# Attention and gated feed-forward on one core: end-of-group work moved between score tiles, row maxima turned on VectorE, weights marked as held

## The chip, the cores and the metric

The kernel runs on one core of one Trainium2 chip. The time of a run is the device time in microseconds (us) of one execution. The engines have the names of the profile: PE (TensorE matmuls), PEld (its weight loads), DVE (VectorE), ACT (ScalarE), POOL (GpSimd) and SP (SyncE, which here only issues DMAs).

## The reference, cut to what matters

```python
x = A_x                                            # 1 x 2048 x 512
mod = (silu(c) @ w_mod).reshape(1, 6, 1, -1)
sa, ca, ga, sb, cb, gb = (mod[:, n] for n in range(6))
h = layernorm(x) * (1 + ca) + sa
q = (h @ wq).reshape(B, S, 32, 16).transpose(0, 2, 1, 3)   # 32 heads of 16
k, v = h @ wk, h @ wv                              # one k and v for all heads
p = softmax(einsum("bhqd,bkd->bhqk", q, k) * 16 ** -0.5)
x = x + ga * (concat_heads(einsum("bhqk,bkd->bhqd", p, v)) @ wo)
h = layernorm(x) * (1 + cb) + sb
x = x + gb * ((sigmoid(h @ w_gate) * (h @ w_up)) @ w_down) # inner width 1792
```

All inputs and the output are float32.

## The kernel before, in words

**Units and steps.** Attention is cut into 32 units: 8 blocks of 256 queries by 4 groups of 8 heads. A unit has 16 steps, one for each block of 128 keys, so the main loop has 512 steps. A step has two half-steps (`for n in range(2)`).

**Scores are computed twice.** A `sa` tile (token `a`, functions `a_tile`, `a_product`, `a_max`) has 128 queries on the partitions and 512 keys along the row; DVE takes its row maximum into `mx`. There are 64 such tiles to a unit, 2048 in all, and they run ahead of the unit that needs them: `A0` of them are done before the main loop starts, and the loop does four per step. An `st` tile (`st_tile`) has 128 keys on the partitions and 512 (query, head) columns; ACT takes its exponential into `P`. The maximum is subtracted inside that product: the rows 48, 49, 112 and 113 of the unit's query tile `qp` hold the maximum, as a high and a low half-precision part, against constant rows of `kp`. So the maxima of a unit must have been turned from partitions into rows, and stored into `qp` by DMA, before the unit's first `st` tile.

**The two halves of the array.** A matmul of the loop uses 64 rows of the PE array and 32 columns; `columns` issues four of them to make 128 columns. In a half-step the two `sa` and the two `st` tiles use one row half (here: the scoring half), and the product of `P` with `V` (`pv`, output `craw`, float32, which runs as two passes) uses the other (the value half). The two halves swap these roles at every second change of step. The order written in a half-step is `ORDER`: `a0 s0 c a1 s1`, where `c` is `pv`.

**Couples.** All the other matrix products (the query projection `pq`, the output projection `po`, gate and up `pgu`, down `pd`) run as a `Couple` of two groups with one PSUM bank each. A couple is cut into parts by `plan`, and `piece` issues one part at the end of a half-step: mostly two terms, each on both row halves (16 matmuls). The last part of a couple calls `end` for both groups. For gate and up these are ACT's `th` (tanh) and DVE's `u` (a copy), for the others likewise one operation on ACT and one on DVE, or two on ACT. They free the couple's two banks, which the next couple needs for its first part, as a rule one half-step later.

**Banks.** PSUM has two banks for `st`, three for `sa`, two for couples and one for `craw`. An `st` tile therefore waits for the exponential of the tile two before it, an `sa` tile for the maximum of the tile three before it.

**Turning the maxima.** When a unit's 64 tiles are reduced, `max_end` (at the start of the next step) reduces `mx` once more in two DVE operations into `m16`; in the step after, `max_rows` turns it with a float32 matmul against `ident` into a bank taken from the `sa` ring, ACT copies it out twice (`m32`, `mh`), and at the end of that step `low` subtracts on DVE and issues four DMAs on SP's queue.

**Order.** Every instruction of PE, DVE, ACT and SP in the loop is kept in the order in which the code issues it (`Ordered`, `keep`). Before the loop a prologue runs from the hand-written list `PLAN`; there `a` issues an `sa` tile and `x` its maximum, `mx`, `my`, `mz` turn the maxima of unit 0.

Of the kernel before, what the change touches and what calls it, by code (L numbers as in the profile page):

```python
# [8 lines left out]
F16 = mybir.dt.float16  # L9
F32 = mybir.dt.float32  # L10
AF = mybir.ActivationFunctionType
ALU = mybir.AluOpType
# [4 lines left out]
P = 128  # L17
# [33 lines left out]
)  # L51

H32 = ('ADAD', 'AAAA', 'AAAA', 'AAAA')
HLO = ('PDPD', 'PPPP', 'PPPP', 'PPPP')

A0 = 84
ORDER = "a0", "s0", "c", "a1", "s1"
LAG = 2

# [37 lines left out]
def adaln_mqa_glu_kernel(  # L97
# [51 lines left out]

    def columns(dst, l_, r_, start, stop):
        for c_ in range(0, P, 32):
            pe.matmul(dst[c_:c_ + 32], l_[:, c_:c_ + 32], r_, start=start, stop=stop)

    turn, done, side, open_ = nc.alloc_semaphore("turn"), [0], [0], [False]
    pe.sem_clear(turn)
# [40 lines left out]
    class Couple:  # L198
# [3 lines left out]
        def part(self, n0, n1):  # L202
            if n0 == 0:
                for g in self.gs:
                    g.open()
            m = self.gs[0].n
            for n in range(n0, n1):
                if n == m:
                    assert self.since is not None or done[0] > self.marks
                    take_over(self.since)  # L210
                for j in (1 - side[0], side[0]):
                    g = self.gs[j ^ (n >= m)]
                    l_, r_, *cut = g.term(n % m, slice(64 * j, 64 * j + 64))
                    columns(cut[0](g.bank) if cut else g.bank, l_, r_, n == 0, n == 2 * m - 1)
                if n == m - 1:
                    self.since, self.marks = None, done[0]
                    if open_[0]:
                        hand_over()
                        self.since = done[0]
                if n in self.after:  # L220
                    self.after[n]()
            if n1 == self.n:
                for k, g in enumerate(self.gs):
                    g.end(g.bank, k == 1)
# [394 lines left out]
    pend, seen = [], {}  # L619

    def max_end(i):
        m16 = wp.tile([64, 32], F32, tag="m16", name="m16", bufs=4)
        for u in range(2):
            dve.tensor_reduce(m16.rearrange("p (h t u) -> p h t u", t=2, u=2)[:, :, :, u], mxs[i][64 * u:64 * u + 64],
                              axis=AX.X, op=ALU.max)
        return lambda: max_rows(i, m16)

    def max_rows(i, m16):
        qp = get_q(i)
        pm = sbank("sa")  # L630
        pe.matmul(pm[:32, :64], m16, ident[:64, :64], start=True, stop=True)
        m32 = wp.tile([32, 64], F32, tag="m32", name="m32", bufs=4)
        act.activation(m32, pm[:32, :64], AF.Identity, scale=1.0 / SM)
        mh = wp.tile([32, 2, 64], F16, tag="mh", name="mh", bufs=4)
        act.activation(mh[:, 0], m32, AF.Identity)

        def low():
            dve.tensor_tensor(mh[:, 1], m32, mh[:, 0], op=ALU.subtract)
            for h in range(2):
                for j in range(2):  # L640
                    r = 64 * j + 48 + h
                    sp1.dma_start(qp[r:r + 1], mh[16 * j:16 * j + 16, h, :])

        return low


    def st_tile(i, t, pr, j, second):
# [191 lines left out]
    def ffn_block(b, end_of_all=False):  # L839
# [63 lines left out]
        def gu_pair(p, t, m):  # L903
            def begin():
                if m == 0:
                    fetched(at + NDC * (p + 1) - 1)

            def term(n, rs):
                k, i = divmod(n, 3)
                h_, w_ = ((0, 0), (1, 0), (0, 1))[i]  # L910
                return h2[t][0][rs, 4 * h_ + k, :], gws[at + NDC * p + k][rs, 2 * w_ + m]

            def end(p_, second):
                if m == 0:
                    ths[p, t] = th = t32("th")
                    act.activation(th, p_, AF.Tanh, scale=0.5 / (SH * SW))
                    return
                u_ = t32("u")
                dve.tensor_copy(u_, p_)
                gated_rows(ths.pop((p, t)), u_, f"g{p}{t}")  # L920

            return Group("gu", 12, "pgu", term, end, begin)

        def gu_last(t):
# [5 lines left out]
            def term(n, rs):  # L930
                k, i = divmod(n, 3)
                gw = gws[at + NDC * NPR + k // 2].rearrange("p m n -> p (m n)")
                h_, w_ = ((0, 0), (1, 0), (0, 1))[i]
                c0 = (2 * (k % 2) + w_) * 512
                return h2[t][0][rs, 4 * h_ + k, :], gw[rs, c0:c0 + 512]

# [143 lines left out]
    def q_end(b, o):  # L1080
# [9 lines left out]
              "a": a_next, "x": lambda: a_max(*held.pop(0)), "mx": lambda: rows.append(max_end(0)), "my": lambda: rows.append(rows.pop()()), "mz": lambda: rows.pop()(),  # L1090
# [73 lines left out]
    def plan(s, hb):  # L1164
# [18 lines left out]
            at += z  # L1183
        assert at == g.n, (at, g.n, g.stage)

    def piece(s, h):
        plan(s, 2 * s + h)
        if run:
# [4 lines left out]


    vq = []
    lows = []

    for i, (b, o) in enumerate(units):
        if o == 0 and b > 0:
# [4 lines left out]
        for kb in range(NKB):  # L1204
# [5 lines left out]
            for z in [z for z in waits if z[0] <= s]:  # L1210
                waits.remove(z)
                z[1]()
            ready_rows, rows[:] = rows[:], [max_end(*z) for z in late]
            an = A0 + 4 * (s - kb % 2)
            second = kb % 2 == 1
            h = sides(kb)[second]

            for n in range(2):
                t = kb - kb % 2 + n
                for z in ORDER:  # L1220
                    k = int(z[1:] or 0)
# [12 lines left out]
            if second:  # L1234
                vq[:] = [(i, kb - 1), (i, kb)]
# [69 lines left out]
```

## Time and profile before

| | |
|---|---|
| time, median of 3 runs | 1634.7 us (1630.74 to 1636.57) |
| profiled execution, its own time | 1629.06 us |
| its span, first to last instruction | 1627.3 us |
| mean granted PE clock | 0.993 |
| PE, PEld busy | 1585.3 us (97%), 987.3 us (61%) |
| DVE, ACT, POOL busy | 1417.1 us (87%), 1288.7 us (79%), 666.2 us (41%) |
| main loop, first to last `st` matmul | 105.1 to 1535.5 us |

In a line of a group stand the code line, the engine, the operation, output and inputs, shapes and count, then busy time and mean duration, then idle time of the engine just before it. Nearly all work is issued through one helper, so its line is L143 and the tile names tell the groups apart. A timeline line has start and length in us; where several alike follow each other they are merged, with their count.

### The profile page before, as it was taken

The page shows a single profiled execution, that of the slowest core. Times are in us where ns is not written, and L with a number is a line of the kernel's source. Part 1 is how long each engine was busy: PE and PEld are TensorE (multiplying, and loading weights), DVE is VectorE, ACT ScalarE, POOL GpSimd, SP SyncE. Part 2 cuts the span into 40 slices and gives each one's busy share as a digit, 9 for nine tenths or more (in the row PEclk, how much of TensorE's full clock was granted, in tenths as well). Part 3 has the DMA queues.
Part 4 walks back from the last instruction along what each step waited for, and adds up shares of the span by engine and source line. Part 5 has one row for each costly group of instructions (what it writes and reads, how often), then busy time and mean ns, then how long its engine had stood idle before and what let it go on. Part 6 is the DMA issues. An engine that isn't in the chain of part 4 may idle for free.

```text
span 1627.3 us, 91846 instructions
## 1 busy us (share of the span) xinstructions
PE 1585.3 (97%) x41481; PEld 987.3 (61%) x41481; DVE 1417.1 (87%) x2400; ACT 1288.7 (79%) x2325; POOL 666.2 (41%) x827
## 2 busy tenths in 40 slices
PE   6899999999999999999999999999999999999998
PEld 3335554546666666666666666666666666665465
DVE  7789999999999999999999999999999999993041
ACT  4539998888888888888888888888888888888600
POOL 5453877244425332443226232543226322533223
PEclk9979999999999999999999999999999999999999
DMA  7122554044521233114321433115411343124411
GB/s 238 71 84 65 164 156 131 28 118 106 139 68 29 75 97 108 31 39 130 92 63 33 89 85 106 30 38 128 112 42 42 81 121 85 23 60 107 116 65 52
DMA packets 185076, 140.22 MB, mean 86 GB/s; under 512 B 96372, under 2 KB 144492, under 8 KB 184684
## 3 DMA queue, kind: packets, MB, share of 16 engines
q1 hardware_dynamic: 184684, 134.34, 30.4%
q8 instruction: 325, 5.32, 1.3%
q14 instruction: 67, 0.55, 0.1%
HBM read 97.18 MB, written 16.24 MB: 70 GB/s over the span
## 4 chain that ended last, share of the span: by engine, by line
PE 88%; DVE 4%; ACT 2%; DMA 2%; POOL 1%; issue 1%; SPq 1%; POOLq 0%; ACTq 0%; DVEq 0%
PE craw L143 24%; PE sa L143 18%; PE pgu L143 17%; PE st L143 11%; PE pd L143 8%; PE po L143 2%; PE pgu L194 2%; PE pq L143 2%; PE pd L194 2%; DVE mx L143 2%; ACT th L143 1%; DMA lc<-lD 1%; SPq L143 1%; DMA xall<-in_A_x_dram 1%; ACT P L143 1%
## 5 line engine op out<-in xcount | busy, mean ns | idle before, releaser
L143 DVE TENSOR_REDUCE mx<-sa 128x1 f32<-128x512 f32 x2048 | 1299.8, 683 | 69.6 <-PE sa L143 33.2
L143 ACT ACTIVATE P<-st 128x512 f32<-128x512 f32 x2048 | 1179.3, 598 | 204.7 <-PE st L143 143.7
L143 PE MATMUL craw<-P,V 64*32 64x512 f32 x8192 | 1086.0, 597 | 1.0 <-ACT cs L143 1.0
L143 PE MATMUL st<-qp,kp 64*32 64x512 f16 x8192 | 832.7, 379 | 7.3 <-ACT P L143 6.1
L143 PE MATMUL sa<-kp,qp 64*32 64x512 f16 (+1 forms) x7940 | 827.9, 378 | 8.2 <-DVE mx L143 6.2
L143 PEld LDWEIGHTS <-kp 64*32 64x32 f16 x8192 | 323.1, 91 | 249.2 <-issue 79.1
L143 PE MATMUL pgu<-gw,h 64*32 64x512 f16 x9408 | 407.4, 376 | 3.2 <-DMA gw<-wD 1.2
L143 PEld LDWEIGHTS <-qp 64*32 64x32 f16 (+1 forms) x7940 | 270.2, 92 | 149.1 <-issue 58.7
L143 PEld LDWEIGHTS <-h 64*32 64x32 f16 (+1 forms) x9600 | 212.7, 92 | 77.8 <-issue 22.6
L143 PEld LDWEIGHTS craw<-P,V 64*32 64x32 f32 x8192 | 184.4, 105 | 21.7 <-issue 2.6
L143 PE MATMUL pd<-wdh,g 64*32 64x512 f16 x2688 | 136.1, 376 | 0.7
L952 POOL TENSOR_SCALAR th<-th 128x512 f32<-128x512 f32 x49 | 30.2, 617 | 246.4 <-ACT th L143 223.2
L569 POOL MEMSET qp<- 32x1024 f16 x60 | 56.7, 944 | 118.6 <-PE st L143 100.5
L143 PEld LDWEIGHTS <-g 64*32 64x32 f16 x4032 | 82.0, 92 | 31.0 <-issue 6.5
L725 POOL TENSOR_TENSOR raw<-raw 128x256 f32<-128x256 f32 x31 | 22.7, 733 | 160.6 <-DMA raw<-lD 151.7
L143 PE MATMUL pd<-wdl,g 64*32 64x512 f16 x1344 | 80.5, 376 | 0.0
L953 POOL TENSOR_TENSOR th<-th,u 128x512 f32<-128x512 f32 x49 | 62.8, 1282 | 4.1
L1009 POOL TENSOR_TENSOR ot<-ot,gb 128x512 f32<-128x512 f32 x12 | 15.4, 1281 | 114.3 <-ACT ot L143 114.3
L143 DVE COPY u<-pgu 128x512 f32<-128x512 f32 (+1 forms) x49 | 31.6, 644 | 34.9 <-PE pgu L143 34.8
L143 PE MATMUL craw<-nought 64*32 64x1 f16 x357 | 58.2, 163 | 1.1 <-issue 1.1
L956 POOL TENSOR_TENSOR gr<-th,gr 128x512 f16<-128x512 f32 x49 | 57.1, 1165 | 4.1
L143 PE MATMUL pq<-h,wdh 64*32 64x512 f16 (+1 forms) x688 | 54.4, 390 | 0.1
(156 smaller groups left out, 1112.5 us busy)
## 6 DMA issues: line engine op xcount, KB each, us to landing
gw<-wD SPq DMA_DIRECT2D x224, 256.0 KB
wD<-gw SPq DMA_DIRECT2D x28, 256.0 KB
wm<-in_w_mod_dram SPq DMA_DIRECT2D x6, 1024.0 KB
qp<-qD SPq DMA_DIRECT2D x192, 32.0 KB
qD<-q SPq DMA_DIRECT2D x16, 256.0 KB
xr<-in_A_x_dram SPq DMA_DIRECT2D x16, 256.0 KB
out_dram<-ot SPq DMA_DIRECT2D x16, 256.0 KB
raw<-cs SPq DMA_DIRECT2D x248, 16.0 KB
```

The costliest lines, as they stand in the source:

```text
L143: return (lambda *a, **k: keep(f_(*a, **k))) if pinned else f_
L194: pe.matmul(cut[0](self.bank) if cut else self.bank, l_, r_, start=(n == 0), stop=(n == self.n - 1))
L569: eng.memset(qp[j:j + 32], 0.0)
L725: keep(pool.tensor_tensor(raw[:, :QU], raw[:, :QU], raw[:, QU:], op=ALU.mult))
L952: pool.tensor_scalar(th, th, 1.0, 1.0, op0=ALU.add, op1=ALU.mult)
L953: pool.tensor_tensor(th, th, u_, op=ALU.mult)
L956: pool.tensor_tensor(rows[:, 1], th, rows[:, 0], op=ALU.subtract)
L1009: pool.tensor_tensor(ot, ot, mods[5], op=ALU.mult)
```

## The change

Four edits.

1. In the half-step that ends a couple (`closes` asks the plan), the part is issued right behind `c`, ahead of `a1` and `s1`, and not after `s1`.
2. The unit maxima are reduced in one DVE operation, split into a high and a low part in two more, and turned by four DVE transpositions of 32x32. The matmul, both ACT copies and the bank go. The four DMAs to `qp` are issued in the middle of the step of `max_end`, one and a half steps earlier in the code than before.
3. `columns` takes `held`: in a part, every third term from the second on is issued with `ldweights=False`, since it has the stationary side of the term ahead of it; for gate and up the terms are put into the order that makes this so.
4. `A0` goes from 84 to 76: the last eight pairs `x a` of `PLAN` go, and each unit's maxima are complete two steps later.

```diff
-A0 = 84
+A0 = 76
...
-    def columns(dst, l_, r_, start, stop):
+    def columns(dst, l_, r_, start, stop, held=None):
         for c_ in range(0, P, 32):
-            pe.matmul(dst[c_:c_ + 32], l_[:, c_:c_ + 32], r_, start=start, stop=stop)
+            if held is None:
+                pe.matmul(dst[c_:c_ + 32], l_[:, c_:c_ + 32], r_, start=start, stop=stop)
+            else:
+                pe.add_instruction(mybir.InstMatmult(
+                    start_tensor_calc=start, stop_tensor_calc=stop, tile_size=(64, 32), tile_position=(held, c_), ldweights=False,
...
-                    columns(cut[0](g.bank) if cut else g.bank, l_, r_, n == 0, n == 2 * m - 1)
+                    columns(cut[0](g.bank) if cut else g.bank, l_, r_, n == 0, n == 2 * m - 1, 64 * j if n % 3 == 1 and n > n0 else None)
...
     def max_end(i):
+        m = wp.tile([P, 16], F32, tag="m", name="m", bufs=2)
+        mm = wp.tile([P, 32], F16, tag="mm", name="mm", bufs=2)
+        mt = wp.tile([32, P], F16, tag="mt", name="mt", bufs=2)
+        dve.tensor_reduce(m, mxs[i].rearrange("p r t k -> p (r t) k"), axis=AX.X, op=ALU.max)
+        dve.tensor_scalar(mm[:, :16], m, 1.0 / SM, None, op0=ALU.mult)
+        dve.scalar_tensor_tensor(mm[:, 16:], m, 1.0 / SM, mm[:, :16], op0=ALU.mult, op1=ALU.subtract)
+        for b in range(0, P, 32):
+            dve.transpose(mt[:, b:b + 32], mm[b:b + 32])
+        return lambda: max_rows(i, mt)
+
+    def max_rows(i, mt):
+        qp = get_q(i)
+        for h in range(2):
+            for j in range(2):
+                r = 64 * j + 48 + h
+                sp1.dma_start(qp[r:r + 1], mt[16 * h + 8 * j:16 * h + 8 * j + 8])
...
-                h_, w_ = ((0, 0), (1, 0), (0, 1))[i]
+                h_, w_ = ((0, 0), (0, 1), (1, 0))[i]
...
+    def closes(s, h):
+        plan(s, 2 * s + h)
+        return bool(run) and run[0][1] > 0 and run[0][1] < run[0][2] == run[0][0].n
...
-            ready_rows, rows[:] = rows[:], [max_end(*z) for z in late]
+            ready_rows = [max_end(*z) for z in late]
...
+                early_ = closes(s, n)
                 for z in ORDER:
...
                     if z == "c" and vq:
                         pv(*vq[n], second)
+                    if z == "c" and early_:
+                        piece(s, n)
                     if z[0] == "s":
                         st_tile(i, t, k, 1 - h, second)
+                if not early_:
+                    piece(s, n)
                 if n == 0:
-                    lows[:] = [z() for z in ready_rows]
-                piece(s, n)
-                if n == 1:
-                    for z in lows:
+                    for z in ready_rows:
                         z()
```

How the built program shows it, at three places. First ACT around the end of a gate-and-up couple late in the loop. The rows are ACT's; `P` is the exponential of an `st` tile (two per half-step), `th` the couple's tanh. Before:

```order
L143 ACTIVATE P_23834<-st 128x512
L143 ACTIVATE P_23852<-st 128x512
L143 ACTIVATE th<-pgu 128x512
L143 ACTIVATE P_23989<-st 128x512
L143 ACTIVATE P_24006<-st 128x512
```

And of the change at the same place:

```order
L143 ACTIVATE P_23781<-st 128x512
L143 ACTIVATE P_23810<-st 128x512
L143 ACTIVATE th<-pgu 128x512
L143 ACTIVATE P_23828<-st 128x512
L143 ACTIVATE P_23965<-st 128x512
```

The tanh stood behind both exponentials of its half-step, and now stands between them. The same holds for DVE's `u` between two `mx`. So it is at 69 ends of couples in the loop.

Second DVE around the maxima of one unit; `mx` are the row maxima of `sa` tiles. Before:

```order
L143 TENSOR_REDUCE mx<-sa 128x1 x4
L143 TENSOR_REDUCE m_22958<-mx 64x16 x2
L143 TENSOR_REDUCE mx<-sa 128x1 x8
L143 TENSOR_TENSOR mh<-m_23085,mh 32x64
L143 TENSOR_REDUCE mx<-sa 128x1 x10
```

And of the change:

```order
L143 TENSOR_REDUCE mx<-sa 128x1 x13
L143 TENSOR_REDUCE m<-mx 128x16
L143 TENSOR_SCALAR mm<-m 128x16
L143 SCALAR_TENSOR_TENSOR mm<-m,mm 128x16
L143 STREAM_TRANSPOSE mt<-mm 32x32 x4
L143 TENSOR_REDUCE mx<-sa 128x1 x9
```

Two operations and, eight `mx` later, a third have become seven in one run, and the run stands eight `mx` later than the first two did.

Third SP's queue around the four DMAs of a unit's maxima, at a place where transposing DMAs (`g<-gr`) come next. Before:

```order
L143 DMA gw<-wD 128x1024 x8
L143 DMA qp<-mh 1x16x64 x4
L143 DMA_TRANSPOSE g_18113<-gr 128x4x128 x2
```

And of the change:

```order
L143 DMA gw<-wD 128x1024 x8
L143 DMA_TRANSPOSE g_18076<-gr 128x4x128
L143 DMA qp<-mt 1x8x128 x4
L143 DMA_TRANSPOSE g_18076<-gr 128x4x128
```

One of the two transposing DMAs now stands ahead of the maxima. On PE the built programs hold the same number of loads for the couples' stationary sides (9600 of `h`, 4032 of `g`, 1344 of `a`, 1032 of `wdh` and `wdl`): the matmuls issued with `ldweights=False` have an LDWEIGHTS ahead of them as the others do.

More of the change, by code (lines that the diff above doesn't have):

```diff
@@ L147, in adaln_mqa_glu_kernel @@
     pool1 = Ordered(nc.gpsimd)
-    def columns(dst, l_, r_, start, stop):
+    def columns(dst, l_, r_, start, stop, held=None):
         for c_ in range(0, P, 32):
-            pe.matmul(dst[c_:c_ + 32], l_[:, c_:c_ + 32], r_, start=start, stop=stop)
+            if held is None:
[3 more added lines that the diff above has]
+                    start_tensor_calc=start, stop_tensor_calc=stop, tile_size=(64, 32), tile_position=(held, c_), ldweights=False,
+                    name=nc.get_next_instruction_name(), engine=mybir.EngineType.PE,
+                    ins=[nc.tensor.lower_ap(r_), nc.tensor.lower_ap(l_[:, c_:c_ + 32])], outs=[nc.tensor.lower_ap(dst[c_:c_ + 32])]))
     turn, done, side, open_ = nc.alloc_semaphore("turn"), [0], [0], [False]
@@ L621, in max_end @@
     def max_end(i):
[L622 to L628, printed above, removed]
-        qp = get_q(i)
[L630 to L644, printed above, removed]
+        m = wp.tile([P, 16], F32, tag="m", name="m", bufs=2)
[8 more added lines that the diff above has]
+    def max_rows(i, mt):
+        qp = get_q(i)
+        for h in range(2):
+            for j in range(2):
+                r = 64 * j + 48 + h
+                sp1.dma_start(qp[r:r + 1], mt[16 * h + 8 * j:16 * h + 8 * j + 8])
     def st_tile(i, t, pr, j, second):
@@ L932, in term @@
                 gw = gws[at + NDC * NPR + k // 2].rearrange("p m n -> p (m n)")
-                h_, w_ = ((0, 0), (1, 0), (0, 1))[i]
+                h_, w_ = ((0, 0), (0, 1), (1, 0))[i]
                 c0 = (2 * (k % 2) + w_) * 512
@@ L1089, in adaln_mqa_glu_kernel @@
               "pm": mod_product, "me": mod_copy, "pr": mod_sum, "m": mod_end,
-              "a": a_next, "x": lambda: a_max(*held.pop(0)), "mx": lambda: rows.append(max_end(0)), "my": lambda: rows.append(rows.pop()()), "mz": lambda: rows.pop()(),
+              "a": a_next, "x": lambda: a_max(*held.pop(0)), "mx": lambda: rows.append(max_end(0)), "my": lambda: rows.pop()(),
               "lw": load_wq, "lx": load_x, "lm": lambda i: load_mod(i, sp1), "bl": lambda: blanks.append(blank(pool1)), "lq": load_q}
@@ L1195, in adaln_mqa_glu_kernel @@
     vq = []
-    lows = []
     for i, (b, o) in enumerate(units):
```

18 rows, old and new, of the table PLAN are left out of this document.

## The prediction

> **What bounds the kernel now.** I read the busy times of the page first, then one stretch of the loop, then the order of time around the end of a couple.
>
> ```profile
> PE 1585.3 (97%) x41481; PEld 987.3 (61%) x41481; DVE 1417.1 (87%) x2400; ACT 1288.7 (79%) x2325; POOL 666.2 (41%) x827
> L143 DVE TENSOR_REDUCE mx<-sa 128x1 f32<-128x512 f32 x2048 | 1299.8, 683 | 69.6 <-PE sa L143 33.2
> 600.00:700.00 100.00, 99.87 (x3013) 66.51 (x3001) 96.81 (x164) 87.82 (x159) 41.31 (x50) 1.00 0.26 66
> L143 PE MATMUL st<-qp,kp x8192: 372/376/631, 105.1 to 1535.5; 64*32 64x512 f16 x200
> ```
>
> The loop's 512 steps take 1430.4 us, 2.79 each, 1.4 a half-step. In a stretch of it PE is busy throughout and DVE for 97%, so neither has room. How they hold each other shows around the end of a gate-and-up couple (times in the text below are within 1096 to 1101):
>
> ```profile
> 1096.68 0.43 PE L143 MATMUL sa<-kp,qp 64*32 64x512 f16 x4
> 1096.76 0.61 PE L143 MATMUL craw<-P,V 64*32 64x512 f32 x4
> 1096.89 0.43 PE L143 MATMUL st<-qp,kp 64*32 64x512 f16 x4
> 1097.11 0.43 PE L143 MATMUL sa<-kp,qp 64*32 64x512 f16 x4
> 1097.19 0.61 PE L143 MATMUL craw<-P,V 64*32 64x512 f32 x4
> 1097.33 0.43 PE L143 MATMUL st<-qp,kp 64*32 64x512 f16 x4
> 1097.43 1.22 ACT L143 ACTIVATE P<-st 128x512 f32<-128x512 f32 x2 [0.33 <-PE st L143]
> 1097.54 0.46 PE L143 MATMUL pgu<-gw,h 64*32 64x512 f16 x7
> 1098.05 0.39 PE L143 MATMUL sa<-kp,qp 64*32 64x512 f16 x3
> 1098.54 0.68 DVE L143 COPY u<-pgu 128x512 f32<-128x512 f32 x1
> 1098.54 0.59 ACT L143 ACTIVATE th<-pgu 128x512 f32<-128x512 f32 x1
> 1098.70 0.42 PE L143 MATMUL st<-qp,kp 64*32 64x512 f16 x4
> 1099.02 1.09 ACT L143 ACTIVATE P<-st 128x512 f32<-128x512 f32 x2
> 1099.19 0.70 PE L143 MATMUL pgu<-gw,h 64*32 64x512 f16 x16
> 1099.62 0.40 PE L143 MATMUL sa<-kp,qp 64*32 64x512 f16 x4
> 1099.83 0.40 PE L143 MATMUL st<-qp,kp 64*32 64x512 f16 x4
> 1100.28 0.60 ACT L143 ACTIVATE P<-st 128x512 f32<-128x512 f32 x1 [0.16 <-PE st L143]
> ```
>
> Four scoring tiles follow each other at 0.215 us (.68, .89, 97.11, .33); meanwhile the other row half does two passes of `craw` at 0.43. Two terms of a couple add 0.43 to both halves, 1.29 in all: both are full. After the couple's end at 1097.54 the next couple's first part comes at 1099.19 and not at 98.92 (0.215 behind the `st` at 98.70): it waits for the bank that `th` leaves at 99.13. The half-step from 1098.05 to 99.62 is 1.57 long, 0.28 over 1.29. That is what edit 1 could save, once per couple.
>
> **Edit 4, 84 to 76.** The prologue ends in a row in which each maximum releases the next tile:
>
> ```profile
> 95.72 10.83 DVE L143 TENSOR_REDUCE mx<-sa 128x1 f32<-128x512 f32 x18
> ```
>
> (10.83 − 0.68) / 17 = 0.60 each. Eight fewer take 4.8 us off. The same eight tiles come back at the end of the loop, in steps that have no `sa` left; there the half with `craw` (0.86) is as full without them, so they cost 0 to 8 × 0.215 = 1.7. Taken: −4.8, ends −6 and −3.
>
> **Edit 2, what goes.** The turning matmul takes scoring time and a bank of the `sa` ring:
>
> ```profile
> 849.28 0.38 PE L143 MATMUL sa<-kp,qp 64*32 64x512 f16 x1
> 850.15 0.21 PE L143 MATMUL sa<-ident,m 64*32 64x64 f32 x1
> 850.59 0.38 PE L143 MATMUL sa<-kp,qp 64*32 64x512 f16 x2
> 852.03 0.40 PE L143 MATMUL sa<-kp,qp 64*32 64x512 f16 x4
> 853.32 0.40 PE L143 MATMUL sa<-kp,qp 64*32 64x512 f16 x4
> ```
>
> The half-steps are 1.31, 1.44 and, free of it, 1.29: 0.17 lost per unit, 31 units in the loop: −5.3 (ends −9 and −3, since both ACT copies go with it).
>
> **Edit 2, what comes.** DVE gets seven operations in a run where it had two, of which none is in the trace in this form. What a run of extra DVE work costs PE shows where two statistics operations stand between maxima:
>
> ```profile
> 506.92 0.68 DVE L143 BATCH_NORM_STATS2 st<-xr 128x6 f32<-128x512 f32 x1
> 507.64 0.18 DVE L143 BATCH_NORM_AGGREGATE mv<-st 128x2 f32<-128x6 f32 x1
> 507.74 3.05 DVE L143 TENSOR_REDUCE mx<-sa 128x1 f32<-128x512 f32 x5
> 507.74 0.39 PE L143 MATMUL sa<-kp,qp 64*32 64x512 f16 x4
> 508.45 0.40 PE L143 MATMUL sa<-kp,qp 64*32 64x512 f16 x4
> 508.65 0.38 PE L143 MATMUL pd<-wdh,g 64*32 64x512 f16 x2
> 508.66 0.37 PE L143 MATMUL st<-qp,kp 64*32 64x512 f16 x1
> 847.09 0.43 DVE L143 TENSOR_REDUCE m<-mx 64x16 f32<-64x64 f32 x2
> ```
>
> They put `mx` off by 0.82 (506.92 to 507.74), and the `sa` tile at 508.45 comes 0.71 behind the one before instead of 0.43: 0.28 lost. So 0.54 of extra DVE work is covered by the ring of three banks, the rest is not. The two `m` of before (0.43) lie under that, so their going gains nothing. The new run: every operation but the later transpositions needs the result of the one ahead, and a dependent one starts 0.04 behind its end (507.60 to 507.64), whereas maxima overlap by 0.08. Start 0.12; reduction 0.21 + 0.04; two small ones and the first wait at 0.18 + 0.04 each, 0.44; four transpositions at 0.10 (from 507.64 to 507.74), 0.40. Sum 1.2, less 0.54 is 0.67, times 31: +20.8. Ends: 0.9 gives +11, transpositions of 0.2 give 1.6 and +33. I take the middle, since small operations are alike in the rows.
>
> **Edit 2 with edit 4, the DMAs.** The maxima now come two steps later and the DMAs at once.
>
> ```profile
> 857.80 0.40 PE L143 MATMUL st<-qp,kp 64*32 64x512 f16 x4
> 95.57 2.53 SPq L143 DMA_DIRECT2D qp<-mh  x4
> 764.25 2.77 DMA qp<-mh
> 1306.79 1.67 DMA qp<-mh
> ```
>
> From `m` (847.09) to the unit's first `st` are 10.7 us; less two steps, 5.1. The run takes 1.2, the last of four issues starts 1.9 later, landing takes 1.7 to 2.8: between 0.3 early and 0.8 late, and the 0.67 by which PE is held ahead of it makes that 1.0 early to 0.1 late. Taken: 0. One transposing DMA that SP now serves first, in some units, is ready long before.
>
> **Edit 1.** The part needs both halves. On the scoring half its two terms stand at 97.11 and 97.33, `a1` at 97.54, `s1` at 97.76. On the other half `craw` lasts until 97.62, so the terms there stay at 97.62 and 97.84: the couple's one group ends 0.43 earlier, its other one no earlier, and ACT and DVE take both ahead of `s1` and `a1`. From an `st` tile to its exponential are 0.45 (99.83 to 100.28), from one ACT operation to the next 0.48 (98.54 to 99.02), its length is 0.60.
> - `th` from the late half: it starts at 97.84 + 0.45 = 98.29, `P` of `s1` at 98.77, ends 99.37. The second `st` of the next half-step takes that bank; it would be due at 98.70 and starts at 99.42: 0.72 lost.
> - `th` from the early half: behind the first `P` at 97.82, `P` of `s1` at 98.30, ends 98.90: 0.25 lost.
>
> Then `u` is the late one, and holds the maximum of `a1` behind it on DVE until 98.29 + 0.60 = 98.89 instead of 97.99; its bank is asked for only three tiles on, after 99.5: covered.
>
> The halves swap, so I take the mean, 0.485. The wait for the couple's bank (0.28) is covered by this longer one and goes. Net +0.21, at 69 places: +14.5. Ends: the bank wait goes and nothing comes, −0.28 × 69 = −19; all from the late half, +0.44 × 69 = +30. For the DVE-and-ACT pairs of `po` and `pd` the same holds.
>
> **Edit 3.** The program still loads ahead of every matmul, so the edit does nothing; new order of terms: the same count. Were the loads gone, it would still be PEld's time beside full row halves: 0.
>
> **Sum.** −4.8 − 5.3 + 20.8 + 0 + 14.5 = +25.2, on the profiled execution's 1629.1: 1654.3. The median of the runs stands 5.6 above that execution, so 1660.
>
> **Rivals.**
> - *Earlier end of the couple pays (faster).* The exponential of `s1` isn't late, so the bank wait of 0.28 goes and nothing comes: −19. With DVE's run at its low end: −4.8 − 5.3 + 11 − 19 = −18, 1617. It decides by whether the second `st` of the half-step after waits for ACT. For it: `th` waits there now. Against: the 0.94 from `s1` (97.76) to that `st` (98.70) are less than 0.45 + 0.60.
> - *The parts cancel.* Edit 1 near nothing and the run near its low end, or edit 1 at −8 and the run as worked out: −4.8 − 5.3 + 11 + 0 = +1, 1636.
> - *Only DVE's run costs.* +10.7, 1645.
> - *The maxima land late.* If the run or SP holds them 1 us longer, PE waits at unit starts, 31 × 0.7 = +22 more: 1682.
> - *The two halves can't run ahead of each other.* Then `a1` waits for the late term at 97.84 and the half-step is 0.22 longer; with `th` early the loss is 0.55, with `th` late still 0.72; net +0.36 × 69 = +25: 1670. Against it stand the rows at 508.65: two `pd` matmuls start ahead of an `st` that is ahead of them in the program, and `craw` at 1096.76 starts before the `st` at 96.89. The Trainium skill's page "TensorE: Matmul & The Clock Gate" (Part 3: Packing small matmuls — row/col tiling) says that matmuls start strictly in program order; by that this rival would be the rule, and the trace does not agree with it.
>
> **How the numbers follow.** From no change this measurement can tell about 0.3%, 5 us. Chances: my forecast (1648 to 1676) 0.48; only DVE's run (to 1648) 0.14; maxima late 0.06; strict order 0.04; cancel 0.12; faster 0.16. So faster 0.16, same 0.12, slower 0.72. The range leaves out a tenth at each side: 1622 to 1680. The forecast's own range is 1648 to 1676.
>
> **What would show it.** DVE: four STREAM_TRANSPOSE per unit near 0.1 to 0.2, and an `sa` tile 1.0 to 1.2 behind the one before it shortly after. ACT: at 69 places `P` of `s1` behind `th`, and an `st` that starts as that `P` ends, the next part without a wait for its bank. PE: no `sa<-ident`, as many LDWEIGHTS of `h`, `g`, `a`. The loop starts near 100 us. Wrong it would be if those `st` don't wait, if the transpositions overlap to nothing, or if the first `st` of units waits for `qp`.

## The result, and the profile after

The changed kernel takes 1672.3 us (median of 6 runs, 1670.8 to 1678.2) against 1633.3 before (6 runs beside it): the ratio is 1.024, with a 95% interval of 1.0215 to 1.0264, so 39 us slower. The prediction was 1660, slower, in a range of 1622 to 1680.

The page and the groups by tile of the kernel after, then its stretch from 600 to 700 (the columns are PE, PEld, DVE, ACT and POOL busy, the granted clock, and the share of the DMA engines):

```profile
span 1668.7 us, 91948 instructions
PE 1607.7 (96%) x41441; PEld 990.9 (59%) x41441; DVE 1444.0 (87%) x2528; ACT 1288.6 (77%) x2261; POOL 666.2 (40%) x827
L143 PE MATMUL st<-qp,kp x8192: 372/376/631, 102.4 to 1577.4; 64*32 64x512 f16 x200
L143 DVE TENSOR_REDUCE mx<-sa 128x1 f32<-128x512 f32 x2048 | 1288.6, 681 | 67.6 <-PE sa L143 32.5
600.00:700.00 100.00, 96.16 (x2808) 61.68 (x2796) 91.67 (x158) 82.38 (x146) 30.61 (x34) 1.00 0.28 77
```

The first `st` comes 2.7 us earlier (102.4, before 105.1), but the loop from the first to the last is 1475.0 long where it was 1430.4: all of the loss lies in it. In the stretch shown PE issued 2808 matmuls where it had issued 3013, and DVE is less busy (91.67, before 96.81): both now wait for each other more. (POOL's 30.61 and 41.31 tell that the two stretches don't hold quite the same steps, so the counts are a sign and no measure.) What PE waited for, in total, number of times and longest, of before and then of after:

```profile
PE sa L143 <- DVE mx L143: 6.2, 15, 1.4
PE st L143 <- ACT P L143: 6.1, 10, 0.9
```

```profile
PE sa L143 <- DVE mx L143: 16.4, 41, 2.0
PE st L143 <- ACT P L143: 15.5, 41, 0.8
PE st L143 <- DMA qp<-mt: 0.8, 2, 0.4
```

Two waits have grown, those that the prediction named: `sa` for DVE (its run) and `st` for the exponential (the early end of couples). The maxima's DMAs hold PE in two units only. The view counts time in which no matmul runs at all; a half that waits beside a busy one isn't in it, so the sums are smaller than the loss.

DVE's run in a typical unit, then the `sa` tiles on PE at the same place:

```profile
964.95 0.21 DVE L143 TENSOR_REDUCE m<-mx 128x16 f32<-128x64 f32 x1
965.20 0.17 DVE L143 TENSOR_SCALAR mm<-m 128x16 f16<-128x16 f32 x1
965.40 0.17 DVE L143 SCALAR_TENSOR_TENSOR mm<-m,mm 128x16 f16<-128x16 f32 x1
965.61 0.84 DVE L143 STREAM_TRANSPOSE mt<-mm 32x32 f16<-32x32 f16 x4
966.39 1.23 DVE L143 TENSOR_REDUCE mx<-sa 128x1 f32<-128x512 f32 x2
```

```profile
965.73 0.41 PE L143 MATMUL sa<-kp,qp 64*32 64x512 f16 x4
967.08 0.40 PE L143 MATMUL sa<-kp,qp 64*32 64x512 f16 x4 [0.18 <-DVE mx L143]
```

From `m` to the next maximum are 1.44 us; the four transpositions take 0.21 each, one behind the other. The `sa` tile behind stands 1.35 after the one ahead of it.

### The profile page after: what moved, and what is told of

The parts are those of the page before. It is cut to its first block, busy times and chain, and to the rows that moved or that the text cites. A ratio compares the mean times of both kernels' runs of the same rounds, so it can differ in the third digit from the quotient of the medians.

```text
span 1668.7 us, 91948 instructions
## 1 busy us (share of the span) xinstructions
PE 1607.7 (96%) x41441; PEld 990.9 (59%) x41441; DVE 1444.0 (87%) x2528; ACT 1288.6 (77%) x2261; POOL 666.2 (40%) x827
## 4 chain that ended last, share of the span: by engine, by line
PE 77%; DVE 10%; ACT 5%; DMA 3%; SPq 2%; issue 2%; POOL 1%; POOLq 0%; ACTq 0%; DVEq 0%
PE craw L143 20%; PE sa L143 15%; PE pgu L143 15%; PE st L143 11%; PE pd L143 7%; DVE mx L143 6%; ACT P L143 3%; PE pgu L200 2%; PE pd L200 2%; PE po L143 2%; SPq L143 2%; PE pq L143 1%; DVE mt L143 1%; DVE mm L143 1%; DMA wst<-in_B_w_gate_dram 1%
## 5 line engine op out<-in xcount | busy, mean ns | idle before, releaser
L143 PE MATMUL pgu<-gw,h 64*32 64x512 f16 x9408 | 437.8, 376 | 2.3 <-issue 1.7
L143 PEld LDWEIGHTS <-qp 64*32 64x32 f16 (+1 forms) x7964 | 276.5, 92 | 163.8 <-issue 77.1
L143 PEld LDWEIGHTS craw<-P,V 64*32 64x32 f32 x8192 | 193.7, 105 | 22.2 <-issue 3.8
L143 PE MATMUL pd<-wdh,g 64*32 64x512 f16 x2688 | 141.5, 376 | 0.0
L143 PE MATMUL pd<-wdl,g 64*32 64x512 f16 x1344 | 85.8, 376 | 0.0
```

The lines of the kernel that those rows point to most:

```text
L143: return (lambda *a, **k: keep(f_(*a, **k))) if pinned else f_
```

## Experiments: the parts one by one

All ratios are to the kernel before, timed beside the kernel in question. "Loop" is the time from the first to the last `st` of the one profiled execution (1430.4 before, 1475.0 after); executions of a kernel scatter by several us, so differences under 5 rest on the ratios. A difference given in us is the ratio's, taken of the time before.

**Edit 1 alone.** Edit:

```
+                early_ = closes(s, n)
...
+                    if z == "c" and early_:
+                        piece(s, n)
...
-                piece(s, n)
+                if not early_:
+                    piece(s, n)
```

> The kernel before with edit 1 alone: the last part of a couple stands between the tiles of s0 and a1, with the couple's evictions issued at that place. My theory (the exponential of s1 queues behind th on ACT, and an st tile a half-step later waits for its bank): +0.21 x 69 = +14.5 us by the prediction, and up to +20 by the traces of after (excess at and behind closings rose from 25.7 to 51.5 us in all, with everything else changed too). Rival, the early end pays: -19. Rival, all of the change's loss is DVE's run: 0, within 3 us. Strict order of the row halves: +25. The trace would show, by my theory, P<-st late behind th at the closings and st waiting for P; by strict order the sa tile of a1 waiting for craw.

Measured: 1654.3, ratio 1.0121 (1.0095 to 1.0146), loop 1450.3: +20 us, more than the +14.5 of the prediction and less than strict order's +25. The timeline around two ends of couples; first one with `th` from the half that ends late, then one with `th` from the half that ends early:

```profile
1127.19 0.38 PE L143 MATMUL st<-qp,kp 64*32 64x512 f16 x4
1127.30 0.41 PE L143 MATMUL pgu<-gw,h 64*32 64x512 f16 x4
...
1127.57 0.69 DVE L143 COPY u<-pgu 128x512 f32<-128x512 f32 x1 [0.28 <-PE st L143]
...
1127.82 0.60 ACT L143 ACTIVATE th<-pgu 128x512 f32<-128x512 f32 x1 [0.39 <-PE pgu L143]
1127.94 0.38 PE L143 MATMUL sa<-kp,qp 64*32 64x512 f16 x1
...
1128.31 1.68 ACT L143 ACTIVATE P<-st 128x512 f32<-128x512 f32 x3
1128.95 0.40 PE L143 MATMUL st<-qp,kp 64*32 64x512 f16 x4 [0.39 <-ACT P L143]
1128.98 0.80 PE L143 MATMUL pgu<-gw,h 64*32 64x512 f16 x16
```

```profile
1109.95 0.43 PE L143 MATMUL pgu<-gw,h 64*32 64x512 f16 x4
1110.05 0.60 ACT L143 ACTIVATE P<-st 128x512 f32<-128x512 f32 x1 [0.33 <-PE st L143]
...
1110.29 0.37 PE L143 MATMUL pgu<-gw,h 64*32 64x512 f16 x1
...
1110.73 0.60 ACT L143 ACTIVATE th<-pgu 128x512 f32<-128x512 f32 x1
...
1111.10 0.42 PE L143 MATMUL sa<-kp,qp 64*32 64x512 f16 x4
...
1111.23 1.68 ACT L143 ACTIVATE P<-st 128x512 f32<-128x512 f32 x3
...
1111.87 0.40 PE L143 MATMUL st<-qp,kp 64*32 64x512 f16 x4
```

In both, `th` stands ahead of the exponential of `s1`, and the `st` that needs that bank starts as the exponential ends (1128.31 + 0.60, 1111.23 + 0.60). In the first it was due 0.215 behind the `sa` at 1127.94, at 1128.16, and comes 0.79 late; in the second due at 1111.32 and 0.55 late. The next couple's part (1128.98) waits no more. The chain is the one predicted. But in the second `th` should have started 0.48 behind `P`, at 1110.53; it starts at 1110.73, 0.44 behind the *other* group's term at 1110.29, which stands ahead of its own last term (1109.95) in the program. And `u` of the first, whose group's last term started at 1126.76, starts only at 1127.57. That gave the question of the next section. (The trace has 73 half-steps with an early end, four more than the 69 of the prediction.)

**Edit 2 alone, edits 2 and 4, edit 3 alone.** The seven operations of the change's `max_end` in place of the old ones with A0 = 84 (the prologue's table then has eight `a x` more); the same with A0 = 76; and the held stationary sides with the new order of terms.

> The kernel before with edit 2 alone: the unit maxima are turned by DVE, A0 stays 84, so the maxima are complete two steps earlier than in the changed kernel. My theory: the run takes about 1.45 us (seen in after), less 0.54 that the sa ring covers is 0.9 x 31 = +28, less the ident matmul's 0.17 x 31 = -5: about +23. Rival, the run is covered better than that, since ACT and PE each lose two operations and one: +5 to +10. Rival, everything is edit 1: -5 to 0.

> Edits 2 and 4 together (the changed kernel without edits 1 and 3). My theory: as the kernel with edit 2 alone, less 2.7 to 4.8 us for the shorter prologue, plus nothing for the DMAs of the maxima: about +19, and with edit 1's +14 to +20 the sum is the changed kernel's +39. Rival, the DMAs of the maxima come late here and hold the first st of each unit: 31 x 0.7 = 22 more than edit 2 alone.

> Edit 3 alone: the order of the three terms of gate, up and down groups and the mark on every third matmul that its stationary side is loaded already. My theory: 0, within 2 us, as many weight loads in the trace as before. Rival: the loads are saved and the row halves run shorter: -5 or more; or the mark makes the weight load wait for the matmul ahead: +5 or more.

Measured: edit 2 alone 1664.3, ratio 1.0186 (1.0155 to 1.0216), loop 1460.4; edits 2 and 4 1657.3, 1.0141 (1.0109 to 1.0174), loop 1459.6; edit 3 1638.6, 1.0024 (1.0003 to 1.0046). So +30, +23 and +4. With edit 1 the sum is 20 + 23 + 4 = 47 against 39 measured together: both large parts are there. Whether some of their waits coincide isn't shown, since edit 3's +4 may be nothing. Edit 3 lies under what I called tellable, with as many loads as before (9600 of `h`, 4032 of `g`, 1344 of `a`); whether its +4 is real stays open.

Edit 4 is worth about 7 beside edit 2 (the two intervals just overlap). Most of that is the prologue. The first `st` of a single execution scatters: it stands at 104.9 to 110.0 in the ten kernels here with A0 = 84 (mean 107.4) and at 100.2 to 102.5 in the three with 76 (mean 101.7). The loops of the two kernels are alike (1460.4 and 1459.6), although they differ in a thing that the prediction had not looked for. DVE and POOL around the run of one unit with A0 = 84:

```profile
907.22 0.21 DVE L143 TENSOR_REDUCE m<-mx 128x16 f32<-128x64 f32 x1
907.38 1.28 POOL L1002 TENSOR_TENSOR ot<-ot,gb 128x512 f32<-128x512 f32 x1
907.46 1.23 DVE L143 TENSOR_SCALAR mm<-m 128x16 f16<-128x16 f32 x1
908.62 2.48 POOL L1008 TENSOR_TENSOR ot<-ot,xr 128x512 f32<-128x512 f32 x2
908.73 1.19 DVE L143 SCALAR_TENSOR_TENSOR mm<-m,mm 128x16 f16<-128x16 f32 x1
909.95 0.84 DVE L143 STREAM_TRANSPOSE mt<-mm 32x32 f16<-32x32 f16 x4
...
911.42 0.40 PE L143 MATMUL sa<-kp,qp 64*32 64x512 f16 x4 [2.06 <-DVE mx L143]
```

The two `mm`, 0.17 elsewhere, take 1.23 and 1.19 and end when POOL's operation ends: the run is 3.5 long, and PE stands for 2.06. By tile (minimum, median and maximum ns), edit 2 alone and then edits 2 and 4:

```profile
L143 DVE TENSOR_SCALAR mm<-m x32: 174/364/1230, 93.1 to 1509.7; 128x16 f16<-128x16 f32 x32
L143 DVE SCALAR_TENSOR_TENSOR mm<-m,mm x32: 174/176/1207, 93.6 to 1510.4; 128x16 f16<-128x16 f32 x32
```

```profile
L143 DVE TENSOR_SCALAR mm<-m x32: 174/175/1082, 94.6 to 1511.3; 128x16 f16<-128x16 f32 x32
L143 DVE SCALAR_TENSOR_TENSOR mm<-m,mm x32: 174/176/1080, 95.1 to 1511.5; 128x16 f16<-128x16 f32 x32
```

With A0 = 76 the run falls where POOL is mostly idle, and the median is the free 175. Counted over the units of edit 2 alone, all 30 `mm` that started with no POOL operation running took 174 to 176 ns; the 34 others took up to 1230, and each of the 31 that were longer than the free ones ended 0.02 to 0.04 behind the end of a POOL operation. The run's mean (from the maximum ahead to the one behind, less 0.60) is 1.99 with A0 = 84 and 1.55 with 76. Why the loop is none the shorter for that is taken up with DVE's run below. The Trainium skill's page "SBUF — State Buffer" (Who interferes with whom) says that VectorE and GpSimd share a port pair as an exclusive lock, which a `tensor_scalar` in a two-port mode and an operation with two SBUF inputs need and a `tensor_reduce` doesn't. The trace agrees: `m` stays at 210 ns and the transpositions at 200 under POOL's work.

## Experiments: what edit 1 costs

**By row half.** The early part issues its terms on the scoring half first, then those on the value half:

```
-            for n in range(n0, n1):
-                for j in (1 - side[0], side[0]):
+            for j in (1 - side[0], side[0]):
+                for n in range(n0, n1):
```

> The kernel with edit 1 alone, in which an early last part is issued by row halves: first its terms on the scoring half, then those on the value half (before they alternate term by term). In the trace of edit 1 alone the group that is finished on the scoring half is taken by ACT or DVE only 0.45 us after the start of the value half's first term (pgu at 1110.29, th at 1110.73), which stands ahead of the group's own last term (1109.95) in the program. Theory: matmuls of the two halves start ahead of each other but their completion is signalled in program order; then issuing the scoring half first lets th start behind P of s0 at 1110.53, 0.2 earlier, in the half of the closings that have th on that side: 35 x 0.2 = 7 us less than edit 1 alone, 1647. Rival: th was late for another reason: as edit 1 alone, 1654 within 3.

Measured: 1653.1, ratio 1.0113 (1.0094 to 1.0132). At the place that corresponds to 1110.73, `th` stands 0.64 behind the last term of its group (0.78 before), so it moved the way it should by 0.14; but 1 us of the time is less than the runs can tell. Inconclusive in time; the table at the end of this section shows it in the half-steps.

**The evictions behind s1.** PE as in edit 1; `th`, `u` and their like are issued behind the exponential and the maximum:

```
+                        ends.append((g, k == 1))
...
+                for g_, k_ in ends:
+                    g_.end(g_.bank, k_)
```

> Edit 1 alone, but the couple's evictions (th, u and the like) are issued behind the exponential of s1 and the maximum of a1; PE's order stays that of edit 1. Theory, the loss is the exponential of s1 queued behind th: then it is gone, and the time is that of before within 5 us (1629 to 1639). Rival, the loss comes from PE's order (two terms of the value half between the tiles, strict starts of the two halves): still 1654.

Measured: 1660.6, ratio 1.0167 (1.0144 to 1.0190): +27, and not back at before. My theory, that the time comes back when `th` leaves its place ahead of the exponential, fell. The timeline of PE, ACT and DVE at the end of a couple in this kernel:

```profile
1137.39 0.39 PE L143 MATMUL st<-qp,kp 64*32 64x512 f16 x4
1137.50 0.41 PE L143 MATMUL pgu<-gw,h 64*32 64x512 f16 x4
...
1138.00 0.69 DVE L143 TENSOR_REDUCE mx<-sa 128x1 f32<-128x512 f32 x1 [0.50 <-PE st L143]
1138.12 0.60 ACT L143 ACTIVATE P<-st 128x512 f32<-128x512 f32 x1 [0.48 <-PE st L143]
...
1138.76 0.40 PE L143 MATMUL st<-qp,kp 64*32 64x512 f16 x4
...
1139.34 0.63 PE L143 MATMUL pgu<-gw,h 64*32 64x512 f16 x16 [0.18 <-DVE u L143]
```

Nothing stands ahead of `P` of `s1` on ACT, which is idle for 0.48, and yet it starts 0.73 behind its `st` (1137.39) and not 0.45. The value half's last term (1137.50) ends at 1137.91; the maximum of `a1` starts 0.09 after that, the exponential 0.21. Both tiles had started before that term, but stand behind it in the program. The next `st` is still late by 0.40, and now the couple's bank is late too: the next couple's part (1139.34) stands 0.58 behind the `st` at 1138.76, where with edit 1 it stood 0.03 behind (1128.98 and 1128.95). So the kernel trades one wait for another, and its time alone doesn't tell what `th` ahead of the exponential costs. The table at the end of this section does.

**Craw behind s1.** Does a matmul's completion reach other engines only when all that stand ahead of it are done, on the other half too? The kernel before, with one table changed:

```
-ORDER = "a0", "s0", "c", "a1", "s1"
+ORDER = "a0", "s0", "a1", "s1", "c"
```

> The kernel before with one table changed: in each half-step the passes of craw are issued behind a1 and s1, not ahead of them (a0, s0, a1, s1, craw, part). In the trace of before, where ACT was idle, the exponential of s0 starts 0.42 to 0.49 us behind the last matmul of its tile, but that of s1 in 80 of 91 cases 0.55 to 0.83 behind, and 0.75 to 0.85 behind the last start of craw. Theory, completion is signalled in program order across the two row halves: with craw issued later, the exponential of s1 starts 0.42 to 0.49 behind its tile; that of s0 is held instead by the value half's last matmuls of the half-step before. Time of the kernel: between 15 less (ACT has the exponential of s1 earlier and the st bank comes free earlier) and 15 more (craw, which frees P, comes later). Rival, the lateness of s1 has another cause (ACT's own queue): the exponential of s1 stays 0.55 to 0.83 behind its tile.

Measured: 1749.0, ratio 1.069 (1.0665 to 1.0715): +114, far outside the ±15 that I gave. The loss isn't time in which PE stands: it waits 5.7 for DVE at `sa` and 2.2 for ACT at `st`, less than in before (6.2 and 6.1). PE has some matmul running for 1714.4 instead of 1585.3, with 41481 matmuls in both. Which order between the halves makes it so wasn't worked out. The latencies answer the question for `s0`. Timeline:

```profile
802.24 0.41 PE L143 MATMUL sa<-kp,qp 64*32 64x512 f16 x4
...
802.46 0.42 PE L143 MATMUL st<-qp,kp 64*32 64x512 f16 x4
802.58 0.40 PE L143 MATMUL pgu<-gw,h 64*32 64x512 f16 x4
...
803.05 1.29 DVE L143 TENSOR_REDUCE mx<-sa 128x1 f32<-128x512 f32 x2 [0.35 <-PE st L143]
...
803.17 1.08 ACT L143 ACTIVATE P<-st 128x512 f32<-128x512 f32 x2 [0.46 <-PE sa L143]
```

The `pgu` at 802.58 belongs to the half-step before and ends at 802.98; `a0` (802.24) and `s0` (802.46) ran ahead of it, and their maximum and exponential start 0.07 and 0.19 behind its end, 0.81 and 0.71 behind their own start. Where ACT had been idle for over 0.1, the exponential of `s0` stood 0.41 to 0.50 behind its tile's last matmul in before (1st to 99th percentile, 530 places); here a quarter of 839 stand 0.64 or more. For `s1` nothing can be told: ACT was idle that long ahead of it at 6 places only. In before `craw` holds `s1` already: 170 of 211 idle places lie at 0.55 to 0.83.

Is it the signal that is late, or only the count that the consumer waits for? All tiles signal on one counter of PE, on which DVE and ACT wait, so the recorded updates of that counter tell. They come at 801.60, 801.82 and 802.03, then none for 0.99, though `a0` and `s0` end within that time, and then three close together at 803.02, 803.08 and 803.14, the first 0.04 behind the end of the `pgu`. So the signals themselves are held back: in this kernel matmuls of the two halves start ahead of each other, and signal in program order. The rule of the Trainium skill's page "PSUM — Partial Sum Buffer" (Engine vs sequencer instructions), that matmuls start and complete in program order, is borne out for the second verb and not for the first.

**Only the scoring half early.** `halves` issues the scoring half's terms at its first call, at the place of edit 1, and the value half's two terms at its second, behind `s1`:

```
+                        two = g_.halves(n0_, n1_)
+                        next(two)
...
+                if early_:
+                    next(two)
```

> Edit 1 alone, with the early last part cut by row half: its terms on the scoring half stand between the tiles as in edit 1, its terms on the value half stand behind s1 as in before (th is evicted early where it is finished on the scoring half; the other evictions come with the value half's terms). Theory, edit 1 costs because the value half's two late terms, ahead of a1 and s1 in the program, hold back the signals of these tiles by about 0.4 us: then most of the +20 goes, 1634 to 1642. Rival, the cost is s1 standing 0.43 closer to the next s1 and th ahead of its exponential, whatever the value half does: 1648 to 1656.

Only where `th` belongs to the scoring half's group does it stand ahead of the exponential of `s1` here; all other evictions stand behind `s1`.

Measured: 1646.9, ratio 1.0067 (1.0046 to 1.0088): +11, between the two. So of edit 1's +20 about 9 go with the value half's terms ahead of `s1` and the evictions that they bring with them, and about 11 with the scoring half's terms and theirs.

What each part does shows at the 42 ends at which a single gate-and-up couple ends. The table has, for each kernel, by how much the second `st` of the next half-step is late (its distance from the first, less 0.43), and the length of that half-step, as means from the traces:

| kernel | 17 ends, `th` from the half that ends late: `st` late, half-step | 25 ends, `th` from the half that ends early: the same |
|---|---|---|
| before | 0.06, 1.61 | 0.04, 1.63 |
| edit 1 | 0.88, 2.15 | 0.61, 1.84 |
| edit 1 by row half | 0.90, 2.17 | 0.47, 1.73 |
| evictions behind `s1` | 0.45, 2.13 | 0.42, 2.11 |
| only the scoring half early | 0.27, 1.84 | 0.44, 1.75 |

Where `th` comes from the late half, the scoring half's terms alone make the `st` 0.27 late: they bring `s1` 0.43 closer to the next `s1`, whose bank it must leave. With the value half's terms ahead of `s1` too, which hold its signal, but no eviction, it is 0.45; with the eviction as well, 0.88. If the parts add, `th` ahead of the exponential is the largest of the three (0.43) and the held signal the smallest (0.18). Where `th` comes from the early half, moving the value half's terms out of its way takes the lateness from 0.61 to 0.47 or 0.44, so the held signal makes 0.14 to 0.17 there.

## Experiments: what DVE's run costs

**The run in four pieces.** With A0 = 84:

```
         dve.tensor_scalar(mm[:, :16], m, 1.0 / SM, None, op0=ALU.mult)
+        yield
         dve.scalar_tensor_tensor(mm[:, 16:], m, 1.0 / SM, mm[:, :16], op0=ALU.mult, op1=ALU.subtract)
         dve.transpose(mt[:, 0:32], mm[0:32])
+        yield
...
```

> Edit 2 alone at A0 = 84, but DVE's run of seven operations is cut into four pieces over four half-steps (m and mm; mm and a transposition; two transpositions; one and the DMAs). In the kernel with edit 2 alone the run takes 1.44 to 3.5 us: 0.12 + 0.24 + 0.21 x 6, and up to 2.5 more where POOL's multiplications and additions of ot are at work (mm from 907.46 lasts 1.23 and ends when POOL's ot ends). Theory: every piece is under the 0.54 that the sa ring covers, so only the held mm operations cost: from before less 5 for the ident matmul to that plus 10, 1629 to 1639. Rival, an operation costs PE its time wherever it stands, since DVE is at 97% in the loop: 31 x 1.45 less what before had (0.43 and one subtraction) = about +25, 1659.

**High parts only.** One reduction writes f16, no `mm`, two DMAs, A0 = 84; the low parts of the maxima stay zero, so what is subtracted ahead of the exponential is coarser:

```
-SM = 16.0
+SM = 1.0
...
+        dve.tensor_reduce(mm[:, :16], mxs[i].rearrange("p r t k -> p (r t) k"), axis=AX.X, op=ALU.max)
         for b in range(0, P, 32):
             dve.transpose(mt[:, b:b + 32], mm[b:b + 32])
```

> Edit 2 alone at A0 = 84, with the maxima rounded to f16 and their low parts left at zero (the shift of the softmax then differs a little, its quotient doesn't): the run is a reduction that writes f16 and four transpositions, no mm operations, two DMAs in place of four. Theory: the two mm operations were the ones that POOL held, so the run takes 0.12 + 0.24 + 4 x 0.21 = 1.2 in every unit; less 0.54, times 31, less 5: +15, 1649. Rival, the reduction and transpositions are held by POOL as well: runs of 2 to 3 us in some units, and more than 1655.

Measured: the pieces 1649.0, ratio 1.0085 (1.0067 to 1.0104); the high parts 1633.7, 0.9992 (0.9977 to 1.0006). Cutting the run takes +30 to +14: the larger part of what costs is not DVE's work as such but its length in one piece. The `mm` are still held by POOL there, 13.2 us in all (mean of the first 433 ns), which is the likely rest. Without `mm` the run is 1.01 to 1.15 in every unit, with no hold, and the time is 15 under what I had expected.

Where the run's cost lies shows when each of a unit's 32 half-steps (from its first `st` to that of the next) is summed over the 32 units and compared with before. Half-steps that no edit touches differ by up to about 2. DVE's run lies in one half-step, at 30 places between maxima in the loop:

| kernel | run, mean | that half-step, longer than before, sum | per run | run less that |
|---|---|---|---|---|
| high parts | 1.02 | 6.2 | 0.21 | 0.81 |
| edits 2 and 4 | 1.55 | 21.2 | 0.71 | 0.84 |
| the changed kernel | 1.62 | 24.4 | 0.81 | 0.81 |
| edit 2 alone | 1.99 | 34.4 | 1.15 | 0.84 |

The last two columns are good to about 0.07. So the `sa` ring covers 0.8 of a run, not the 0.54 of the prediction, and PE pays for what is longer one for one. The matmul against `ident` stood in the 27th half-step of a unit. Where the run lies elsewhere, the 27th and 28th together are 7.3 shorter than before (edits 2 and 4), 7.8 (the changed kernel) and 6.9 (the three pieces with A0 = 76, below): that is what its going gains. With the high parts alone the run's 6.2 and a gain of 6.4 in the three half-steps behind it cancel.

One thing stays open. With edits 2 and 4 the loop is 29 longer, of which +21.2 and -7.3 are accounted for. The other 15 lie elsewhere, 7.7 of them in the two half-steps behind the run (in the changed kernel 9.0, of which edit 1 alone has 3.2). That is why its loop is as long as with edit 2 alone, in spite of the shorter run.

**The high parts in three pieces, A0 = 76 and 80.**

```
-A0 = 84
+A0 = 76     # in the second kernel 80
```

> Candidate: edits 2 and 4 without edits 1 and 3, the maxima rounded to f16 with the low parts left at zero, and DVE's run (a reduction and four transpositions) cut into three pieces over three half-steps, A0 = 76. In the kernel with the high parts alone the run of 1.03 us cost 0.26 a unit, the ident matmul's going gained 0.17; pieces of 0.45 or less should cost 0.1 a unit or nothing. From 1634: -5 for the ident matmul, -3 to -5 for the shorter prologue, +0 to +3 for the pieces: 1624 to 1632. Rival, the DMAs come too late for the unit's first st, as A0 = 76 leaves 2 us: +10 or more, above 1636.

> Candidate: as the kernel with the high parts spread over three half-steps, but A0 = 80: the maxima of a unit are then complete in its twelfth step, as with 84, two steps earlier than with 76, so the two DMAs land in time. In the kernel with A0 = 76 the first st of each unit waited 0.6 to 1.0 us for them: 31 x 0.8 = 25 goes; the prologue is 4 x 0.60 = 2.4 shorter than with 84. From the kernel with the high parts alone at 84 (1633.7): -2.4 for the prologue and -3 to -8 for the pieces (0.26 a unit for the run in one piece): 1624 to 1629, against 1635 before. Rival: the pieces cost as much as the run: 1631 or more.

Measured: 1654.9, ratio 1.0114 (1.0080 to 1.0149), with 76; 1629.8, 0.9977 (0.9959 to 0.9994), with 80. With 76 the DMAs come late; the waits view and a unit's start:

```profile
PE st L143 <- DMA qp<-mt: 15.3, 24, 1.0
```

```profile
957.44 0.62 SPq L143 DMA_DIRECT2D qp<-mt  x1
959.65 0.40 PE L143 MATMUL st<-qp,kp 64*32 64x512 f16 x4 [0.82 <-DMA qp<-mt]
```

The last DMA is issued 1.4 ahead of the time at which the `st` was due and lands 2.2 after its issue: the two half-steps that the pieces take are more than the maxima had to spare. With 80 a unit's maxima are complete as early as with 84, and the wait is gone. That kernel is 0.2% faster than before, which is less than I called tellable, with the coarser maxima. Its loop is no shorter than before's (1431.4), so what gain there is lies ahead of it, and the going of the ident matmul bought no more than the new pieces cost.

## Why the prediction came out as it did

- **Direction and the two causes: right.** Slower, by DVE's run and by the early end of couples, each shown alone. The forecast's own range (1648 to 1676) holds 1672, but the sum was +25 and not +39.
- **Edit 1, +14.5, measured +20: the chain right, the early half too small.** The `st` that waits for `P` behind `th` is there. For `th` from the late half the half-step was to be 0.44 longer and is 0.54; for `th` from the early half it was to be 0.03 shorter and is 0.21 longer. The step that failed is in "*`th` from the early half*: behind the first `P` at 97.82": it lost 0.25 there and the traces show 0.61. Its group isn't signalled when it ends but when the other half's term ahead of it in the program ends, and the signal of `s1` is held likewise. The rival "the two halves can't run ahead of each other" was set aside because starts do; what it says holds of the signals, and its 0.55 for `th` early was nearer than the forecast's 0.25. The held signal is about 0.15 of the 0.36 that were missing; the rest of them is open.
- **Edit 2, what comes, +20.8, measured 24.4: near, by two errors that partly cancel.** The first is "four transpositions at 0.10 (from 507.64 to 507.74)": that was the overlap of a small operation with a maximum, and small ones behind each other take 0.21. The run is 1.45 and not 1.2 where POOL is idle, and POOL's hold on `mm`, which the sum didn't have at all, makes it 1.62 in the mean. The second is the cover of 0.54, which is 0.8. So that this term came out near was luck.
- **Edit 2, what goes, -5.3, measured 7 to 8: right**, within its ends of -9 and -3.
- **What no term had:** about 6 in the two half-steps behind the run that edit 1 alone doesn't have; the cause is open.
- **Edit 4, -4.8: right.** The means of the first `st` are 5.7 apart. The prologue ends as predicted in one `mx` per 0.60:

```profile
96.01 9.05 DVE L143 TENSOR_REDUCE mx<-sa 128x1 f32<-128x512 f32 x15
```

- **DMAs late, 0: right** for this kernel (0.8 us in two units), but with nothing to spare, as A0 = 76 with the pieces shows.
- **Edit 3, 0: within what can be told.**

## What to carry to other kernels

Here a matmul that ran ahead of the other row half still reported behind it. So when you order two halves, look for a long or late matmul of one that stands ahead, in the program, of a tile that another engine waits for. Then measure the new order whole: putting `craw` behind `s1` for that reason cost 114 us, and putting the evictions behind the exponential only moved the wait to the couple's bank. Short operations on a full engine are paid by the length of the run they form, beyond what the ring of banks covers (0.8 us here), so cut the run or drop an operation, and see what POOL does meanwhile. Each piece takes time from the deadline of what it feeds; move the deadline first.

## What the runs showed of the hardware

- Matmuls on different row halves start out of program order (`st` at 802.46 ahead of `pgu` at 802.58), but their consumers start 0.07 to 0.21 behind the end of the earlier one in the program, up to 0.8 behind their own start. PE's counter had no update between 802.03 and 803.02, then three within 0.12.
- 32x32 f16 transpositions on DVE take 0.20 each and follow at 0.21; they don't overlap, while the maximum behind them starts 0.06 before their end.
- A DVE operation of 0.17 took up to 1.23 while POOL ran; reductions (0.21) and transpositions (0.20) beside the same POOL work did not change.
